# The half-wide pair of a fused attention and double-FFN kernel: operations on two tiles, another product order, one store for two batches

## The chip, the cores and the metric

One core of a Trainium2 chip. The metric is the device time of one execution in microseconds, the median of three runs. The profile is of one further execution of the same program.

## The reference, cut to what matters

All in float32; three stages, the output of each is the input of the next.

```
kv  = einsum('bhsd,bhse->bhde', k, v);  o = einsum('bhsd,bhde->bhse', q, kv)      # batch 8, heads 8, seq 576, dim 64
x   = o / sqrt(mean(o*o, -1) + 1e-6) * g_norm          # as 4608 x 512
x1  = max(x @ w1, x @ w2, x @ w3) @ w_out              # 768 hidden columns
out = (s * relu(x1 @ w_in)**2 + b) @ moe2_w_out        # 2048 hidden columns, 512 out
```

The change lies in the last product, with the `w_out` of the third stage.

## The kernel before, in words

Numbers are kept as pairs of a high and a low part (`hi_part`, a ScalarE copy that rounds, L290; `lo_part`, a VectorE subtraction of that copy from the number, L293), and a product is three matmuls: high by high, high by low, low by high. The two products of the third stage are done with Strassen's method in Winograd's form, with seven products i = 0 to 6 for eight.

The tokens are columns. They are worked on in five pairs of token blocks q; the first four pairs hold two batches' first 512 rows each, in blocks of N = 512 columns. The remaining 64 rows of each of the eight batches (REM = 64) are gathered in a ninth block of 512 columns, and the fifth pair (q = 4) is this block, cut into two halves of 256 columns. `width(q)` says which. This is the half-wide pair. For the last product the work on a pair goes through two halves of the contraction, H = 2q and 2q + 1; so H = 8 and 9 belong to the half-wide pair.

For each H and each of its products i, four steps k of the contraction: `z_load` brings the hidden tiles back from DRAM (`gd`) through SP's queue; `z_sum` makes the sums that products 2 and 3 need, in place, in the tiles of i = 1; `z_hi` and `z_lo` make the high and low part in a slot `zx`, one of six (the tags HS); `z_product` runs 2 x 3 matmuls a step, two output halves m by three part products, into PSUM banks a, b or c (products 0, 2, 4, 6 accumulate in a, 1 and 3 in b, 5 in c). In the half-wide pair a slot holds two steps side by side, 256 columns each, and each m has a bank of its own of which it uses half. `z_comb` takes the banks out: for i < 3 a ScalarE copy, and, where H is odd, VectorE adds what the even H left; for i = 3, 4, 5 VectorE adds bank and copy; for i = 6 it adds to what stands there; at an odd H ScalarE then applies `s` and the bias for each m.

At an odd H, `plan_put` brings the result out. For the first four pairs VectorE transposes a tile in 32 x 32 blocks (`put`, L1255) into one of the four tiles of the rings `t` and `st`, and `put_store` writes it with four DMAs of 64 KB (L1267), each to a destination seen as `a r f` with a = 4 outermost. For the half-wide pair TensorE turns the tile by a product with a unit matrix (`turn_mm`, L1272, for c = 0, 1 and u = 0, 1: tiles named xho and xlo), ScalarE copies it out (`turn_out`, L1277), and `turn_store` (L1282) writes each of the tile's two batches with a DMA of 64 rows by 2 KB, so eight in all; the second of a tile of c = 1 is issued from ScalarE, all others from SP.

The order of the work on every engine is fixed when the program is built. Each piece of work is entered with `job(pos, engine, cost, ...)`: a place in the list, a cost in microseconds, the names that it reads and writes, and the ring slots that it takes. `arrange` plays the list through: an engine takes, of the jobs that are ready when it is free, the one with the lowest place; a job is ready when those that it depends on have ended by the given costs and a lag (2.0 for SP, 0.1 for others, 3.0 for loads). The order so found is what each engine's queue gets; on the chip each engine then runs its queue in that order and waits where it must. `SIZE` gives the slots of a ring. So a cost that is off moves no work on the chip by itself, but changes which work stands before which.

Of the kernel before, what the change touches and what calls it, by code (L numbers as in the profile page):

```python
# [30 lines left out]
def attention_max_ffn_relu2_ffn(ctx: ExitStack, tc, q, k, v, g_norm, w1, w2, w3, wo, wi, w2o, s, b, out):  # L31
# [257 lines left out]
    def hi_part(out, src):  # L289
        act(out=out, in_=src, func=AF.Copy)  # L290
# [566 lines left out]
    def width(q):  # L857
        return N if q < NQ - 1 else N // 2
# [218 lines left out]
    def z_load(H, i, u):  # L1077


        q, n = H // 2, width(H // 2)  # L1080
        parts = (0, 1) if n < N else (H % 2,)
        t = ring("c", f"z_{H}_{u}") if i == 1 else slot(GS[i][u], f"z_{H}_{i}_{u}", F32)
        for e in parts:
            c = slice(e * n, (e + 1) * n) if n < N else slice(0, N)
            k0 = 4 * e
            h = 2 * q + e
            if i == 1:
                p2["z", h, 1, u] = t[:, c]
                nc.sync.dma_start(out=t[:, c], in_=gd[q][:, 3, k0 + u, :n])
                continue  # L1090
            nc.sync.dma_start(out=t[:, :, c], in_=gd[q][:, KEPT[i], k0 + 2 * u:k0 + 2 * u + 2, :n])
            for m in range(2):
                p2["z", h, i, 2 * u + m] = t[:, m, c]

    def z_tile(H, i, k_):
        H0 = H if width(H // 2) == N else H // 2 * 2
        return f"Z{H0}.{i}.{k_ if i == 1 else k_ // 2}"

    def z_key(H, i, k_):
        return f"{z_tile(H, i, k_)}:{0 if i == 1 else k_ % 2}{H % 2}"  # L1100

    def plan_z_load(pos, H, i, u):
        q = H // 2
        k = [u] if i == 1 else [2 * u, 2 * u + 1]
        parts = (0, 1) if width(q) < N else (H % 2,)
        job(pos, SQ_, 0.85 * len(k), z_load, H, i, u, r=[f"gd{q}:{3 if i == 1 else KEPT[i]}.{4 * e + k_}" for e in parts for k_ in k],
            w=[z_key(2 * q + e, i, k_) for e in parts for k_ in k], a=[("c" if i == 1 else GS[i][u], z_tile(H, i, k[0]))], lag=3.0)

    def z_x(H, i, k_):
        return f"ZX{28 * H + 4 * i + (k_ if width(H // 2) == N else k_ // 2 * 2)}:{k_ % 2}"  # L1110

    def z_sum(H, i, k_):
        z = lambda i_: p2["z", H, i_, k_]
        if i == 2:
            tt(nc.vector, z(1), z(1), add, z(0))
        else:
            tt(nc.vector, z(1), z(5), sub, z(1))

    def z_hi(H, i, k_):
        n, o = width(H // 2), 28 * H + 4 * i + k_  # L1120
        if n == N or k_ % 2 == 0:
            st["zx", H, i, k_ // 2] = slot(HS[(o if n == N else o // 2) % M1], f"zx_{o}")
        c = slice(0, N) if n == N else slice(k_ % 2 * n, (k_ % 2 + 1) * n)
        x = hs["z", H, i, k_] = st["zx", H, i, k_ // 2][:, :, c]
        hi_part(x[:, 0], p2["z", H, 1 if 0 < i < 4 else i, k_])

    def z_lo(H, i, k_, eng):
        x = hs["z", H, i, k_]
        lo_part(x[:, 1], p2["z", H, 1 if 0 < i < 4 else i, k_], x[:, 0], nc.gpsimd if eng == G_ else nc.vector)

    def plan_z_right(pos, H, i, k_):
        n, o = width(H // 2), 28 * H + 4 * i + k_
        z = lambda i_: z_key(H, i_, k_)
        if i in (2, 3):
            job(pos, V, cost(V, n), z_sum, H, i, k_, r=[z(0 if i == 2 else 5)], w=[z(1)])
        f, x = z(1 if 0 < i < 4 else i), z_x(H, i, k_)
        new = n == N or k_ % 2 == 0
        job(pos, A, cost(A, n), z_hi, H, i, k_, r=[f], w=[x + "h"],
            a=[(HS[(o if n == N else o // 2) % M1], x.split(":")[0])] if new else [])
        eng = V  # L1140
        job(pos, eng, cost(eng, n), z_lo, H, i, k_, eng, r=[f, x + "h"], w=[x + "l"])

    def z_product(H, i, k_):
        n, new = width(H // 2), i in (0, 1, 5)
        kk = 4 * (H % 2) + k_
        w, x = wt["q", 4 + kk // 2, i], hs["z", H, i, k_]
        for m in range(2):
            if new and k_ == 0:
                st["ps", "z", H, BANK[i], m] = bank(parity(H + (i == 5)), f"zs_{BANK[i]}_{H}_{m}")
            ps = st["ps", "z", H, BANK[i], m][:, :n]  # L1150
            c = slice((2 * (kk % 2) + m) * P, (2 * (kk % 2) + m + 1) * P)
            for e, (a, b_) in enumerate(((0, 0), (0, 1), (1, 0))):
                nc.tensor.matmul(ps, lhsT=w[:, a, c], rhs=x[:, b_], start=new and k_ == 0 and e == 0,  # L1153
                                 stop=k_ == 3 and e == 2, skip_group_check=True)

    def plan_z_product(pos, H, i, k_):
        names = [f"Y{BANK[i]}{H}.{m}" for m in range(2)]
        g = 4 + (4 * (H % 2) + k_) // 2
        job(pos, "PE", 1.365 if width(H // 2) == N else 0.72, z_product, H, i, k_,
            r=[f"WQ{g}.{i}:0", f"WQ{g}.{i}:1", z_x(H, i, k_) + "h", z_x(H, i, k_) + "l"], w=names,  # L1160
            a=[(parity(H + (i == 5)), nm) for nm in names] if i in (0, 1, 5) and k_ == 0 else [])

    def acc(H, i_, m):
        c = int(i_ in (4, 6))
        if ("o", H // 2, c) not in p2:
            tg = ("xh", "xl")[c]
            p2["o", H // 2, c] = base.tile([P, KD, N], F32, tag=tg, name=f"{tg}o_{H}")
        return p2["o", H // 2, c][:, 2 * (i_ in (3, 4)) + m, :width(H // 2)]

    def z_comb(H, i, m, e):  # L1170
        n = width(H // 2)
        ps = st["ps", "z", H, BANK[i], m][:, :n]
        if e == 0:
            st["zc", H, i, m] = ring("s", f"zc_{H}_{i}_{m}")[:, :n]
            act(out=st["zc", H, i, m], in_=ps, func=AF.Copy)
        elif e == 1:
            s_ = st["zc", H, i, m]
            tt(nc.vector, s_, s_, add, acc(H, 5 - i, m))
        elif e == 2:
            tt(nc.vector, acc(H, i, m), ps, add, st["zc", H, 5 - i, m])  # L1180
        elif e == 3:
            tt(nc.vector, acc(H, i, m), ps, add, acc(H, i, m))
        elif e == 4:
            act(out=acc(H, i, m), in_=ps, func=AF.Copy)
        else:
            b_ = 2 * (i in (3, 4)) + m
            act(out=acc(H, i, m), in_=acc(H, i, m), func=AF.Identity, scale=sb_s, bias=p2["bias"][:, b_:b_ + 1])

    def plan_z_combine(pos, H, i):
        n, more = width(H // 2), H % 2  # L1190
        o = lambda i_, m: f"O{H // 2}.{int(i_ in (4, 6))}:{2 * (i_ in (3, 4)) + m}"
        for m in range(2):
            ps = f"Y{BANK[i]}{H}.{m}"
            if i < 3:
                c = f"ZC{H}.{i}.{m}"
                job(pos, A, cost(A, n), z_comb, H, i, m, 0, r=[ps], w=[c], a=[("s", c)])
                if more:
                    job(pos, V, cost(V, n), z_comb, H, i, m, 1, r=[o(5 - i, m)], w=[c])
                continue
            c = int(i in (4, 6))  # L1200
            new = [(("xh", "xl")[c], f"O{H // 2}.{c}")] if not more and m == 0 and i in (3, 4) else []
            e = 2 if i < 6 else 3 if more else 4
            eng = A if e == 4 else V
            job(pos, eng, cost(eng, n), z_comb, H, i, m, e, r=[ps] + ([f"ZC{H}.{5 - i}.{m}"] if e == 2 else []), w=[o(i, m)], a=new)
            if more:
                job(pos, A, cost(A, n), z_comb, H, i, m, 5, r=["bias"], w=[o(i, m)])

# [67 lines left out]
        act(out=o.rearrange("p (a m r) -> p m a r", a=4, m=4), in_=st["turn", c, u].rearrange("p (m a r) -> p m a r", a=4, m=4),  # L1277
            func=AF.Copy)

    def turn_store(c, u, e, eng):  # L1280
        r0 = (4 * c + 2 * u + e) * S_ + N
        (nc.scalar if eng == A else nc.sync).dma_start(out=out[r0:r0 + REM], in_=st["put", c, u][e * REM:(e + 1) * REM])  # L1282

    def plan_put(pos, H, c, u):
        q = H // 2
        tag = either()
        o = [f"O{q}.{c}:{i}" for i in range(4)]
        nm = f"R{H}.{c}.{u}"
        if q < NQ - 1:
            job(pos, V, 0.78, put, H, c, u, tag, r=o, w=[nm], a=[(tag, nm)])  # L1290
            job(pos + 0.05, SQ_, 1.4, put_store, H, c, u, r=[nm])
            return
        job(pos, "PE", 1.0, turn_mm, c, u, r=[*o, "unit"], w=["T" + nm], a=[(parity(u), "T" + nm)])
        job(pos + 0.01, A, 0.65, turn_out, c, u, tag, r=["T" + nm], w=[nm], a=[(tag, nm)])
        for e in range(2):
            eng = A if c and e else SQ_
            job(pos + 0.02, eng, 0.6, turn_store, c, u, e, eng, r=[nm])

# [239 lines left out]
    job(T4 + 28 * (NQ - 1) + 1, G_, 1.0, unit, w=["unit"], a=[("c", "unit")])  # L1540
    for H in range(2 * NQ):
        t = T4 + 14 * H
        order = (0, 5, 1, 2, 3, 4, 6) if H == 2 * NQ - 1 else range(7)
        for n, i in enumerate(order):
            for kk in range(4):
                plan_z_right(t + 2 * n + 0.5 * kk - 3, H, i, kk)
# [37 lines left out]
```

## Time and profile before

| | |
|---|---|
| time, median of 3 runs | 1358.96 us (1358.86 to 1359.13) |
| profiled execution | 1358.27 us |
| its span, first to last instruction | 1356.5 us |
| TensorE (PE) busy | 1336.8 us, 99% of the span |
| VectorE (DVE) busy | 982.4 us, 72% |
| ScalarE (ACT) busy | 788.0 us, 58% |
| mean granted TensorE clock | 0.999 |
| moved by DMA | 251.81 MB, mean 186 GB/s |

The span is the profiled execution from its first to its last instruction; 1.8 us of the execution lie outside of it. Busy shares are means over stages that have different limits; the windows and timelines below cut them into stages.

### The profile page before, as it was taken

The numbers are of one execution on the slowest core, as the hardware profiler recorded it, in microseconds if no ns is written. First come the engines' busy times: TensorE is split into PE (matmuls) and PEld (weight loads), VectorE is DVE, ScalarE is ACT, GpSimd is POOL, SyncE is SP. The second block draws the span as 40 slices with busy tenths as digits, with TensorE's granted clock in tenths as the row PEclk, the third lists the DMA queues.
The fourth block names the chain that finished last, engine by engine and source line by source line (L and its number), as shares of the span: only waits on it lengthen the run. The fifth ranks groups of instructions, "written<-read, shape, count | busy, mean of one in ns | idle before, by whom it ended". The sixth has DMA issues, their size and how long they took to land.

```text
span 1356.5 us, 19727 instructions
## 1 busy us (share of the span) xinstructions
PE 1336.8 (99%) x6948; PEld 1102.0 (81%) x6948; DVE 982.4 (72%) x1671; ACT 788.0 (58%) x1399; POOL 68.1 (5%) x58
## 2 busy tenths in 40 slices
PE   7999999999999999999999999999999999999998
PEld 4777777778888888878888889888888888888888
DVE  4994666767658885477647768658888888888875
ACT  6873555556435453165546567567775656566565
POOL 0001212123110000000000000000000000000000
PEclk9999999999999999999999999999999999999999
DMA  9988988753527638575535645436584464554531
GB/s 267 298 181 210 221 215 224 209 157 95 152 87 249 240 117 267 205 244 184 177 149 196 238 174 169 172 139 223 194 307 151 142 211 142 178 164 138 182 113 48
DMA packets 241010, 251.81 MB, mean 186 GB/s; under 512 B 119184, under 2 KB 177552, under 8 KB 238736
## 3 DMA queue, kind: packets, MB, share of 16 engines
q1 hardware_dynamic: 240752, 250.31, 59.9%
q8 instruction: 54, 0.88, 0.3%
q14 instruction: 44, 0.36, 0.1%
q10 hardware_dynamic: 160, 0.26, 0.1%
HBM read 149.85 MB, written 100.66 MB: 185 GB/s over the span
## 4 chain that ended last, share of the span: by engine, by line
PE 95%; DVE 2%; DMA 1%; SPq 1%; ACT 1%; issue 0%; ACTq 0%; DVEq 0%
PE ps_a L999 15%; PE zs_a L1153 14%; PE g L161 10%; PE g L163 9%; PE g L162 9%; PE ps_b L999 7%; PE fp_a L1392 7%; PE zs_b L1153 7%; PE zs_c L1153 4%; PE ps_c L999 4%; PE fp_b L1392 4%; PE fp_c L1392 2%; PE kvor L348 1%; PE ops L417 1%; PE ms L456 1%; DMA vrem<-in_v_dram 1%
## 5 line engine op out<-in xcount | busy, mean ns | idle before, releaser
L290 ACT ACTIVATE zx<-z 128x512 fp32r<-128x512 f32 (+1 forms) x280 | 158.4, 586 | 122.6 <-PE zs_a L1153 37.8
L1153 PE MATMUL zs_a<-zx,w_q 128*128 128x512 f32 (+1 forms) x960 | 210.9, 368 | 1.0 <-DVE zx L293 1.0
L293 DVE TENSOR_TENSOR zx<-z,zx 128x512 fp32r<-128x512 f32 (+1 forms) x280 | 171.3, 634 | 53.6 <-ACT zx L290 50.2
L999 PE MATMUL ps_a<-x_q,w_q 128*128 128x512 f32 (+1 forms) x960 | 206.0, 368 | 0.0
L1153 PEld LDWEIGHTS zs_a<-zx,w_q 128*128 128x128 f32 x960 | 168.2, 189 | 31.2 <-DVE zx L293 1.2
L999 PEld LDWEIGHTS ps_a<-x_q,w_q 128*128 128x128 f32 x960 | 167.8, 189 | 29.9
L161 PE MATMUL g<-xh,w_w 128*128 128x512 f32 x360 | 142.6, 396 | 0.0
L163 PE MATMUL g<-xh,w_w 128*128 128x512 f32 x360 | 140.4, 390 | 0.7 <-DVE w_w L293 0.7
L162 PE MATMUL g<-xl,w_w 128*128 128x512 f32 x360 | 140.3, 390 | 0.0
L1153 PE MATMUL zs_b<-zx,w_q 128*128 128x512 f32 (+1 forms) x480 | 108.5, 368 | 1.9 <-DVE zx L293 1.9
L999 PE MATMUL ps_b<-x_q,w_q 128*128 128x512 f32 (+1 forms) x480 | 105.1, 368 | 0.0
L1153 PEld LDWEIGHTS zs_b<-zx,w_q 128*128 128x128 f32 x480 | 84.5, 188 | 17.3 <-DVE zx L293 2.3
L999 PEld LDWEIGHTS ps_b<-x_q,w_q 128*128 128x128 f32 x480 | 84.2, 189 | 15.0
L161 PEld LDWEIGHTS g<-xh,w_w 128*128 128x128 f32 x360 | 67.5, 188 | 15.6 <-issue 0.8
L163 PEld LDWEIGHTS g<-xh,w_w 128*128 128x128 f32 x360 | 67.6, 188 | 15.5 <-DVE w_w L293 1.1
L162 PEld LDWEIGHTS g<-xl,w_w 128*128 128x128 f32 x360 | 67.6, 188 | 13.7 <-DVE xl L293 0.3
L576 DVE TENSOR_TENSOR h<-g,h 128x512 f32<-128x512 f32 x60 | 41.5, 691 | 38.5 <-PE g L163 37.3
L1028 ACT ACTIVATE cs<-cs 128x512 f32<-128x512 f32 (+1 forms) x60 | 35.1, 586 | 53.5 <-DVE cs L855 52.8
L1400 ACT ACTIVATE fc<-fp_a 128x512 f32<-128x512 f32 x36 | 21.4, 597 | 68.4 <-PE fp_a L1392 66.0
L1015 ACT ACTIVATE cs<-ps_a 128x512 f32<-128x512 f32 (+1 forms) x80 | 43.4, 555 | 24.9 <-PE ps_a L999 21.0
L1153 PE MATMUL zs_c<-zx,w_q 128*128 128x512 f32 (+1 forms) x240 | 54.1, 368 | 0.0
L855 DVE TENSOR_TENSOR cs<-ps_b,cs 128x512 f32<-128x512 f32 (+1 forms) x40 | 24.9, 637 | 39.5 <-issue 32.5
(325 smaller groups left out, 2498.9 us busy)
## 6 DMA issues: line engine op xcount, KB each, us to landing
z<-gd SPq DMA_DIRECT2D x64, 512.0 KB
gd<-cs SPq DMA_DIRECT2D x96, 256.0 KB
z<-gd SPq DMA_DIRECT2D x48, 256.0 KB
x1d<-x SPq DMA_DIRECT2D x36, 256.0 KB
sd<-fs SPq DMA_DIRECT2D x18, 512.0 KB
raw_w<-in_moe_w_dram SPq DMA_DIRECT2D x18, 511.0 KB
k<-in_k_dram SPq DMA_DIRECT2D x32, 256.0 KB
v<-in_v_dram SPq DMA_DIRECT2D x32, 256.0 KB
```

The source lines that it names most:

```text
L161: nc.tensor.matmul(ps, lhsT=w[:, 0, sl], rhs=xh, start=first, stop=False)
L162: nc.tensor.matmul(ps, lhsT=w[:, 0, sl], rhs=xl, start=False, stop=False)
L163: nc.tensor.matmul(ps, lhsT=w[:, 1, sl], rhs=xh, start=False, stop=last)
L290: act(out=out, in_=src, func=AF.Copy)
L293: eng.tensor_tensor(out=out, in0=src, in1=hi.bitcast(F32), op=ALU.subtract)
L576: nc.vector.tensor_tensor(out=st["h", m], in0=ps, in1=st["h", m], op=ALU.max)
L855: eng.tensor_tensor(out=out, in0=in0, in1=in1, op=op)
L999: nc.tensor.matmul(ps, lhsT=w[:, a, c], rhs=x[:, b_], start=new and k == 0 and e == 0, stop=k == HK - 1 and e == 2, skip_group_check=True)
L1015: act(out=st["cs", G, i, m], in_=st["ps", G, BANK[i], m][:, :n], func=AF.Copy)
L1028: act(out=h, in_=st["ps", G, BANK[i], m][:, :width(q)] if i == 6 else h, func=AF.Relu)
L1153: nc.tensor.matmul(ps, lhsT=w[:, a, c], rhs=x[:, b_], start=new and k_ == 0 and e == 0, stop=k_ == 3 and e == 2, skip_group_check=True)
L1392: nc.tensor.matmul(ps, lhsT=w[:, u, c], rhs=x[:, v_], start=new and k == 0 and e == 0, stop=k == HK - 1 and e == 2, skip_group_check=True)
```

## The change

The half-wide pair only, but for one number.

- `z_load`: for i = 1, a tile holds two steps of one H instead of one step of both, and comes with one DMA in place of two.
- `z_sum`, `z_hi`, `z_lo`: one operation on the two steps k of a slot (128 x 512 elements) in place of two on 128 x 256.
- `z_product`, `z_comb`: both m share one PSUM bank, 256 columns each, and one operation takes both out. The scaling with the bias stays one for each m.
- The product order of H = 8 is 0, 1, 5, 2, 4, 3, 6; it was 0 to 6. That of H = 9 is as before.
- `turn_store`: one DMA a tile for its two batches, four in all; that of c = 1, u = 1 is issued from ScalarE.
- The list's cost of `put_store` is 2.6 for 1.4, that of `turn_store` 0.7 for 0.6. The first holds for all pairs.

```diff
@@ z_load
+            if i == 1 and n < N:
+                if u // 2 == e:
+                    t2 = p2["zp", h, 1, u % 2] = t.rearrange("p (m n) -> p m n", m=2)
+                    nc.sync.dma_start(out=t2, in_=gd[q][:, 3, k0 + u % 2 * 2:k0 + u % 2 * 2 + 2, :n])
+                continue
@@ z_hi
+        if n < N:
+            x2 = st["zx", H, i, k_ // 2]
+            for m in range(2):
+                hs["z", H, i, k_ + m] = x2[:, :, m * n:(m + 1) * n]
+            hi_part(x2[:, 0].rearrange("p (m n) -> p m n", m=2), p2["zp", H, 1 if 0 < i < 4 else i, k_ // 2])
+            return
@@ z_product
-            if new and k_ == 0:
+            if new and k_ == 0 and (n == N or m == 0):
                 st["ps", "z", H, BANK[i], m] = bank(parity(H + (i == 5)), f"zs_{BANK[i]}_{H}_{m}")
-            ps = st["ps", "z", H, BANK[i], m][:, :n]
+            ps = st["ps", "z", H, BANK[i], m] if n == N else st["ps", "z", H, BANK[i], 0][:, m * n:(m + 1) * n]
@@ z_comb
-        ps = st["ps", "z", H, BANK[i], m][:, :n]
+        ps = st["ps", "z", H, BANK[i], m if n == N else 0]
+        if n < N:
+            ps = ps.rearrange("p (m n) -> p m n", m=2)
@@ plan_z_combine
-        for m in range(2):
+        for m in (0, 1) if full else (None,):
@@ turn_store
-    def turn_store(c, u, e, eng):
-        r0 = (4 * c + 2 * u + e) * S_ + N
-        (nc.scalar if eng == A else nc.sync).dma_start(out=out[r0:r0 + REM], in_=st["put", c, u][e * REM:(e + 1) * REM])
+    def turn_store(c, u, eng):
+        to = out.rearrange("(b s) d -> b s d", s=S_)[4 * c + 2 * u:4 * c + 2 * u + 2, N:]
+        (nc.scalar if eng == A else nc.sync).dma_start(out=to, in_=st["put", c, u])
@@ plan_put
-            job(pos + 0.05, SQ_, 1.4, put_store, H, c, u, r=[nm])
+            job(pos + 0.05, SQ_, 2.6, put_store, H, c, u, r=[nm])
...
-        for e in range(2):
-            eng = A if c and e else SQ_
-            job(pos + 0.02, eng, 0.6, turn_store, c, u, e, eng, r=[nm])
+        job(pos + 0.02, A if c and u else SQ_, 0.7, turn_store, c, u, A if c and u else SQ_, r=[nm])
@@ the list
-        order = (0, 5, 1, 2, 3, 4, 6) if H == 2 * NQ - 1 else range(7)
+        order = (0, 5, 1, 2, 3, 4, 6) if H == 2 * NQ - 1 else (0, 1, 5, 2, 4, 3, 6) if H == 2 * NQ - 2 else range(7)
```

## Rows read from the trace of the kernel before

**Rows 1.** Windows: busy us of PE, PEld, DVE, ACT, POOL; clock; DMA share; GB/s.
```profile
34.00:995.00 961.00, 958.78 (x4958) 786.29 (x4958) 672.60 (x1126) 546.01 (x963) 65.86 (x48) 1.00 0.63 194
...
1299.50:1325.00 25.50, 22.56 (x167) 21.16 (x167) 21.70 (x55) 15.73 (x43) 0.00 (x0) 1.00 0.28 83
...
1345.60:1356.50 10.90, 6.23 (x51) 5.76 (x49) 0.79 (x2) 3.90 (x8) 0.00 (x0) 0.91 0.38 96
```

**Rows 2.** Timeline of PE, 1309 to 1319: start, length, work, idle before and its releaser.
```profile
1309.41 2.44 PE L1153 MATMUL zs_a<-zx,w_q 128*128 128x256 f32 x19
1312.86 0.86 PE L1153 MATMUL zs_a<-zx,w_q 128*128 128x256 f32 x5 [1.01 <-DVE zx L293]
1313.56 1.00 PE L1153 MATMUL zs_b<-zx,w_q 128*128 128x256 f32 x7
1315.96 1.57 PE L1153 MATMUL zs_b<-zx,w_q 128*128 128x256 f32 x11 [1.41 <-DVE zx L293]
...
1318.09 0.28 PE L1153 MATMUL zs_b<-zx,w_q 128*128 128x256 f32 x1
1318.90 0.86 PE L1153 MATMUL zs_b<-zx,w_q 128*128 128x256 f32 x5 [0.53 <-DVE zx L293]
```

**Rows 3.** Timeline of DVE: the first and the last of three waiting transposes.
```profile
1311.79 0.71 DVE L1255 STREAM_TRANSPOSE o<-xlo 128x512 f32<-128x512 f32 x1 [0.71 <-DMA out_dram<-o]
...
1317.82 0.71 DVE L1255 STREAM_TRANSPOSE o<-xlo 128x512 f32<-128x512 f32 x1 [0.91 <-DMA out_dram<-o]
```

**Rows 4.** Groups by line and form, 1220 to 1357: count, busy us, mean ns, idle before.
```profile
L293 DVE TENSOR_TENSOR zx<-z,zx 128x512 fp32r<-128x512 f32 x57 | 38.4, 688 | 12.3 <-ACT zx L290 11.4
L290 ACT ACTIVATE zx<-z 128x512 fp32r<-128x512 f32 x57 | 35.2, 630 | 28.0 <-PE zs_a L1153 9.0 <-DVE zx L293 5.8 <-PE zs_b L1153 5.0
...
L293 DVE TENSOR_TENSOR zx<-z,zx 128x256 fp32r<-128x256 f32 x56 | 20.5, 415 | 5.3 <-ACT zx L290 5.0
L290 ACT ACTIVATE zx<-z 128x256 fp32r<-128x256 f32 x56 | 20.1, 411 | 15.7 <-PE zs_a L1153 4.8 <-PE zs_b L1153 4.3 <-issue 2.8
```

**Rows 5.** Timeline of SP's queue: the stores of H = 7.
```profile
1303.04 23.03 SPq L1267 DMA_DIRECT2D out_dram<-o  x32
```

**Rows 6.** DMA view, 1306 to 1324: GB/s in 40 slices; queue's packets, MB, share.
```profile
GB/s 77 69 68 101 72 68 85 83 86 82 84 92 82 86 86 85 86 86 86 86 86 86 86 86 86 86 86 86 86 86 86 86 86 122 88 85 86 86 85 88
...
q1 hardware_dynamic: 3032, 1.51, 28.4%
```

**Rows 7.** DMA view, 1345.6 to 1356.5, slices of 0.27 us: busy tenths, GB/s.
```profile
DMA  0000000039799100000000897979993797900000
GB/s 0 0 0 0 0 0 0 0 90 233 165 233 203 38 0 0 0 0 0 0 0 8 210 225 188 218 188 210 188 346 143 188 180 218 368 8 0 0 0 0
```

**Rows 8.** DMA view, 1266 to 1272: two large loads of `z`.
```profile
DMA  2100000000000000000276569999999620000000
GB/s 82 55 27 0 0 0 0 0 0 0 0 0 0 0 0 0 0 0 0 68 123 109 130 232 335 362 362 341 382 369 382 212 89 0 0 0 0 0 0 0
```

**Rows 9.** Timeline of all engines, 1344 to 1357.
```profile
1344.80 1.05 PE L1272 MATMUL turn<-unit,xho 128*128 128x128 f32 x8
...
1345.61 3.12 PE L1153 MATMUL zs_a<-zx,w_q 128*128 128x256 f32 x24
...
1346.76 6.70 SPq L1282 DMA_DIRECT2D out_dram<-ot  x6
1348.40 0.79 DVE L855 TENSOR_TENSOR xlo<-zs_a,xlo 128x256 f32<-128x256 f32 x2 [2.97 <-PE zs_a L1153]
...
1348.56 1.06 PE L1272 MATMUL turn<-unit,xho 128*128 128x128 f32 x8
1348.86 1.09 ACT L1187 ACTIVATE xlo<-xlo,lim,sb_s 128x256 f32<-128x256 f32 x2 [2.13 <-DVE xlo L855]
...
1351.61 0.58 ACTq L1282 DMA_DIRECT2D out_dram<-ot  x1
1352.36 0.60 ACT L1277 ACTIVATE ot<-turn 128x512 f32<-128x512 f32 x1 [0.79 <-PE turn L1272]
```

More of the change, by code (lines that the diff above doesn't have):

```diff
@@ L1091, in z_load @@
             nc.sync.dma_start(out=t[:, :, c], in_=gd[q][:, KEPT[i], k0 + 2 * u:k0 + 2 * u + 2, :n])
+            if n < N:
+                p2["zp", h, i, u] = t[:, :, c]
             for m in range(2):
@@ L1096, in z_tile @@
         H0 = H if width(H // 2) == N else H // 2 * 2
-        return f"Z{H0}.{i}.{k_ if i == 1 else k_ // 2}"
+        return f"Z{H0}.{i}.{k_ // 2 if i != 1 else k_ if width(H // 2) == N else 2 * (H % 2) + k_ // 2}"
     def z_key(H, i, k_):
@@ L1103, in plan_z_load @@
         q = H // 2
-        k = [u] if i == 1 else [2 * u, 2 * u + 1]
-        parts = (0, 1) if width(q) < N else (H % 2,)
+        half = width(q) < N
+        k = [u] if i == 1 and not half else [2 * (u % 2), 2 * (u % 2) + 1]
+        parts = ((u // 2,) if i == 1 else (0, 1)) if half else (H % 2,)
         job(pos, SQ_, 0.85 * len(k), z_load, H, i, u, r=[f"gd{q}:{3 if i == 1 else KEPT[i]}.{4 * e + k_}" for e in parts for k_ in k],
-            w=[z_key(2 * q + e, i, k_) for e in parts for k_ in k], a=[("c" if i == 1 else GS[i][u], z_tile(H, i, k[0]))], lag=3.0)
+            w=[z_key(2 * q + e, i, k_) for e in parts for k_ in k], a=[("c" if i == 1 else GS[i][u], z_tile(2 * q + parts[0], i, k[0]))], lag=3.0)
     def z_x(H, i, k_):
@@ L1112, in z_sum @@
     def z_sum(H, i, k_):
-        z = lambda i_: p2["z", H, i_, k_]
+        z = lambda i_: p2["z", H, i_, k_] if width(H // 2) == N else p2["zp", H, i_, k_ // 2]
         if i == 2:
@@ L1122, in z_hi @@
             st["zx", H, i, k_ // 2] = slot(HS[(o if n == N else o // 2) % M1], f"zx_{o}")
-        c = slice(0, N) if n == N else slice(k_ % 2 * n, (k_ % 2 + 1) * n)
-        x = hs["z", H, i, k_] = st["zx", H, i, k_ // 2][:, :, c]
+        if n < N:
[4 more added lines that the diff above has]
+            return
+        x = hs["z", H, i, k_] = st["zx", H, i, k_ // 2]
         hi_part(x[:, 0], p2["z", H, 1 if 0 < i < 4 else i, k_])
     def z_lo(H, i, k_, eng):
+        if width(H // 2) < N:
+            hi, lo = (st["zx", H, i, k_ // 2][:, e].rearrange("p (m n) -> p m n", m=2) for e in range(2))
+            lo_part(lo, p2["zp", H, 1 if 0 < i < 4 else i, k_ // 2], hi, nc.vector)
+            return
         x = hs["z", H, i, k_]
@@ L1132, in plan_z_right @@
         n, o = width(H // 2), 28 * H + 4 * i + k_
-        z = lambda i_: z_key(H, i_, k_)
+        if n < N and k_ % 2:
+            return
+        ks = (k_,) if n == N else (k_, k_ + 1)
+        z = lambda i_: [z_key(H, i_, k) for k in ks]
         if i in (2, 3):
[L1135 to L1141, printed above, removed]
+            job(pos, V, 0.69, z_sum, H, i, k_, r=z(0 if i == 2 else 5), w=z(1))
+        f, x = z(1 if 0 < i < 4 else i), [z_x(H, i, k) for k in ks]
+        job(pos, A, 0.62, z_hi, H, i, k_, r=f, w=[x_ + "h" for x_ in x], a=[(HS[(o if n == N else o // 2) % M1], x[0].split(":")[0])])
+        job(pos, V, 0.69, z_lo, H, i, k_, V, r=f + [x_ + "h" for x_ in x], w=[x_ + "l" for x_ in x])
     def z_product(H, i, k_):
@@ L1147, in z_product @@
         for m in range(2):
-            if new and k_ == 0:
+            if new and k_ == 0 and (n == N or m == 0):
                 st["ps", "z", H, BANK[i], m] = bank(parity(H + (i == 5)), f"zs_{BANK[i]}_{H}_{m}")
-            ps = st["ps", "z", H, BANK[i], m][:, :n]
+            ps = st["ps", "z", H, BANK[i], m] if n == N else st["ps", "z", H, BANK[i], 0][:, m * n:(m + 1) * n]
             c = slice((2 * (kk % 2) + m) * P, (2 * (kk % 2) + m + 1) * P)
             for e, (a, b_) in enumerate(((0, 0), (0, 1), (1, 0))):
-                nc.tensor.matmul(ps, lhsT=w[:, a, c], rhs=x[:, b_], start=new and k_ == 0 and e == 0,
+                nc.tensor.matmul(ps, lhsT=w[:, a, c], rhs=x[:, b_], start=new and k_ == 0 and e == 0 and (n == N or m == 0),
                                  stop=k_ == 3 and e == 2, skip_group_check=True)
     def plan_z_product(pos, H, i, k_):
-        names = [f"Y{BANK[i]}{H}.{m}" for m in range(2)]
+        names = [f"Y{BANK[i]}{H}.{m}" for m in range(2 if width(H // 2) == N else 1)]
         g = 4 + (4 * (H % 2) + k_) // 2
@@ L1167, in acc @@
             p2["o", H // 2, c] = base.tile([P, KD, N], F32, tag=tg, name=f"{tg}o_{H}")
+        if m is None:
+            return p2["o", H // 2, c][:, 2 * (i_ in (3, 4)):2 * (i_ in (3, 4)) + 2, :width(H // 2)]
         return p2["o", H // 2, c][:, 2 * (i_ in (3, 4)) + m, :width(H // 2)]
@@ L1171, in z_comb @@
         n = width(H // 2)
-        ps = st["ps", "z", H, BANK[i], m][:, :n]
+        ps = st["ps", "z", H, BANK[i], m if n == N else 0]
+        if n < N:
+            ps = ps.rearrange("p (m n) -> p m n", m=2)
         if e == 0:
-            st["zc", H, i, m] = ring("s", f"zc_{H}_{i}_{m}")[:, :n]
+            st["zc", H, i, m] = ring("s", f"zc_{H}_{i}_{m}")
+            if n < N:
+                st["zc", H, i, m] = st["zc", H, i, m].rearrange("p (m n) -> p m n", m=2)
             act(out=st["zc", H, i, m], in_=ps, func=AF.Copy)
@@ L1189, in plan_z_combine @@
     def plan_z_combine(pos, H, i):
-        n, more = width(H // 2), H % 2
-        o = lambda i_, m: f"O{H // 2}.{int(i_ in (4, 6))}:{2 * (i_ in (3, 4)) + m}"
-        for m in range(2):
-            ps = f"Y{BANK[i]}{H}.{m}"
+        more, full = H % 2, width(H // 2) == N
+        for m in (0, 1) if full else (None,):
+            o = lambda i_: [f"O{H // 2}.{int(i_ in (4, 6))}:{2 * (i_ in (3, 4)) + m_}" for m_ in ((m,) if full else (0, 1))]
+            ps = f"Y{BANK[i]}{H}.{m or 0}"
             if i < 3:
                 c = f"ZC{H}.{i}.{m}"
-                job(pos, A, cost(A, n), z_comb, H, i, m, 0, r=[ps], w=[c], a=[("s", c)])
+                job(pos, A, 0.62, z_comb, H, i, m, 0, r=[ps], w=[c], a=[("s", c)])
                 if more:
-                    job(pos, V, cost(V, n), z_comb, H, i, m, 1, r=[o(5 - i, m)], w=[c])
+                    job(pos, V, 0.69, z_comb, H, i, m, 1, r=o(5 - i), w=[c])
                 continue
             c = int(i in (4, 6))
-            new = [(("xh", "xl")[c], f"O{H // 2}.{c}")] if not more and m == 0 and i in (3, 4) else []
+            new = [(("xh", "xl")[c], f"O{H // 2}.{c}")] if not more and not m and i in (3, 4) else []
             e = 2 if i < 6 else 3 if more else 4
             eng = A if e == 4 else V
-            job(pos, eng, cost(eng, n), z_comb, H, i, m, e, r=[ps] + ([f"ZC{H}.{5 - i}.{m}"] if e == 2 else []), w=[o(i, m)], a=new)
+            job(pos, eng, 0.62 if e == 4 else 0.69, z_comb, H, i, m, e, r=[ps] + ([f"ZC{H}.{5 - i}.{m}"] if e == 2 else []), w=o(i), a=new)
             if more:
-                job(pos, A, cost(A, n), z_comb, H, i, m, 5, r=["bias"], w=[o(i, m)])
+                for m_ in (m,) if full else (0, 1):
+                    job(pos, A, cost(A, width(H // 2)), z_comb, H, i, m_, 5, r=["bias"], w=[f"O{H // 2}.{c}:{2 * (i in (3, 4)) + m_}"])
     def bias_load(g):
```

## The prediction

> **What bounds the kernel now.** I read the windows first. From 34 to 995 us TensorE is busy 958.78 of 961.00 us, and the stages after it up to 1299.5 have no gap at all, so nothing there can be won from another engine. Two places are left: in 1299.5 to 1325 TensorE is busy 22.56 of 25.50 us, and after 1345.6 it is busy only 6.23 of 10.90 us [rows 1]. The clock is not the matter: it is granted in full until the last window.
>
> Then the timeline of TensorE for the first place. It stops three times, each time for VectorE's low part of a `zx` tile [rows 2]. A half-wide matmul starts every 0.12 us (24 of them fill 1345.61 to 1348.56, [rows 9]). So 19 of them from 1309.41 last until 1311.69 and the next starts at 1312.86: 1.17 us lost; in the same way 1.56 us before 1315.96 and 0.69 us before 1318.90, together 3.4 us.
>
> VectorE's timeline tells why: three of its transposes (first and last shown) wait 0.71, 1.08 and 0.91 us for a store of `out` to land, and the `zx` operations queue behind them [rows 3]. The list gave such a store 1.4 us; SP's queue spends 23.03 us on eight of them, 2.9 us each [rows 5], and the ring holds four tiles. While they run, the DMA view is flat at 86 GB/s with 28.4% of the 16 engines in use, although SP issues the next one as fast as it can [rows 6].
>
> **The change part by part.**
>
> Operations on two tiles. In the pair H=8, 9 there are 56 high and 56 low parts of 128x256; 28 and 28 of 128x512 take their place. VectorE: 56 x 0.415 = 23.2 us becomes 28 x 0.688 = 19.3; ScalarE: 56 x 0.411 = 23.0 becomes 28 x 0.630 = 17.6 [rows 4]. The 16 sums and 20 combinations on VectorE halve likewise; at the same durations 36 x 0.415 = 14.9 becomes 18 x 0.688 = 12.4. That is 6.4 us of VectorE, which is not on the path except in the stretch of the three stops, and it pays with latency: high and then low part of the first tile take 1.3 us where 0.83 did.
>
> The product order. For H=8 it becomes 0, 1, 5, 2, 4, 3, 6. Product 5 needs no sum, so it gives VectorE a product's time (24 x 0.12 = 2.9 us) in which to do the late transposes. Its price: a slot of `zx` is (28H+4i+k)//2 mod 6, so products 5 and 2 of H=8 both get slots 2 and 3. Product 2's first tiles can be made only when 5's first two k are done, 0.63 + 0.69 us plus hand-overs, about 1.4 us, beside the 1.44 us that 5's other two k take. That fits with nothing to spare; a transpose that waits for its store there goes straight to TensorE.
>
> The store's time in the list: 2.6 us for 1.4. No instruction comes or goes; the last four transposes move back by 1.2 us a store, near to where their tiles come free. The list still lands each store too early: it gives 2.6 us where 2.9 were seen, and its landing is assumed. So some waiting stays. Of the 3.4 us I take 2.0 as won (bounds: all 3.4, or none).
>
> The loads. For i=1 eight loads of 128 KB become four of 256 KB. SP's last `z` load is out well before 1303.04 [rows 5] and the three stops name no load, so this is worth nothing; were it uncovered, it could only save issues.
>
> PSUM. Both halves of a product share one bank, so one operation reads both and must wait for the second. At the end this costs: now VectorE starts on the first half at 1348.40 while TensorE finishes the second [rows 9]. Then it starts 0.37 us later and takes 0.69 for 0.42: ScalarE's two scalings come 0.6 us later. The fewer banks also free one early for the second turn of `xho`, which now runs at 1348.56 beside the last combination; by its place in the list it goes ahead of product 6 and adds its 0.9 us to TensorE. The first turn and its ScalarE copy are late by some 0.3 us, as product 3's combination takes both halves at once.
>
> The turned stores. This decides. Eight stores of 128 KB become four of 256 KB, one a tile. It saves issues: ScalarE no longer issues a store at 1351.61 between its two last copies, 0.5 us of the 0.79 us idle before 1352.36 [rows 9]. But the destination is now `out` as (batch, row, column) with 2 batches outermost; before it was 64 rows. The rows show two stores that differ in this: the one at L1267, whose destination has 4 outermost, moves 86 GB/s with 28.4% of the engines in use [rows 6], no more than four and a half engines, however many are queued; the present turned stores, with 64 outermost, move 180 to 230 GB/s with nearly all engines busy [rows 7]. I read this as: a store is dealt out over as many engines as its outermost size lets it, and consecutive stores use the same ones. With 2 outermost each engine gets 128 KiB of a store.
>
> The Trainium skill, page "DMA: Bandwidth & Descriptors", section "Why a DMA increments its semaphore by 16 and not by 1", says it outright: a transfer runs on the largest number of engines, at most 16, that divides the slowest dimension above 1 of both sides, and on SP's and ScalarE's queues on the lowest-numbered ones. By it a store of 2 outermost runs on two engines, and ScalarE's store lands on the same two as SP's; no row here shows a store of 2 outermost, nor ScalarE's queue beside SP's on few engines. Without that rule the reading from rows 6 and 7 gives the same two engines.
>
> The price: an engine moves 21.5 GB/s in rows 6 (86 over 4) and 21.3 to 23.9 in the full slices of a large load (341 to 382 over 16, [rows 8]). I take 23.2. Four stores are 4 x 131,072 bytes an engine, 22.6 us (bounds 21.9 to 24.6). They start with the first: its issue at 1346.76 moves by -2.0 + 0.3 to 1345.1, the first bytes come 1.0 us later (1346.76 to the ninth slice of rows 7, 1347.8), so the data ends at 1346.1 + 22.6 = 1368.7. The later stores are issued some 1 and 5 us after the first, always while the two engines are still busy, so what happens to TensorE behind the first store costs and gains nothing any more. From the last bytes to the end of the span it is 1.1 us (1355.4 to 1356.5): 1369.8, which is 13.3 us more than 1356.5. The profiled execution took 1358.27, 0.7 under the median shown; its sum gives 1371.6, and on the median of 1358.96 it is **1372**.
>
> **The rivals.**
>
> All engines (not slower): the lowering deals the store out by the 128 partitions of the source, or by rows. Against it: the store of L1267 has 128 partitions as its source too, and stays at 86 GB/s. Then the path is TensorE's: -2.0 (stops) + 0.9 (second turn) + 0.6 (last combination) - 0.5 (ScalarE's issue) = -1.0, **1358**. It would be below 1356.2 only with all the stops gone and the second turn still behind product 6. It decides at eight engines or more: then a store takes 1.4 us and is under the present tail.
>
> Each store on a pair of its own: two engines a store, but different ones. Against it: the flat 86 GB/s of successive stores. Then only the last store counts: its issue at 1352.99 - 2.0 + 0.9 + 0.6 - 0.5 = 1352.0, bytes from 1353.0, 5.65 us, 1.1 us: 1359.8, 3.3 us more, **1362**.
>
> The stops grow (the change does not do what it says), with all engines: products 5 and 2 share slots, and one transpose that waits between them, 1.1 us as in rows 3, and a `zx` behind it, bring as much as they save, so the 3.4 us stay and the tail's +1.0 comes on top with the slot chain's 1 us: **1361**. For it: the list still sets a landing too early. Under the forecast it only moves the first store, by 2 us, to 1374.
>
> **How the numbers follow.** Forecast 0.82, all engines 0.11 (0.08 within 0.2%, 0.03 faster), own pairs 0.05, stops grow 0.02 (2.0 us, within 0.2%). 0.2% is 2.7 us, about what a measurement of this kernel can tell from no change. Slower: 0.82 + 0.05 = 0.87; same 0.08 + 0.02 = 0.10; faster 0.03. Of the forecast alone the low end is all stops gone and the fastest rate, 1343.4 + 1.0 + 21.9 + 1.1 = 1367.4, 1370 as a time; the high end no gain, the second turn and the slowest rate, 1347.9 + 1.0 + 24.6 + 1.1 = 1374.6, 1377. The engines alone may run faster than in a crowd, so I go down to 1366.
>
> **What would show it.** Right: after about 1350 the DMA view falls to some 45 GB/s at an eighth of the engines, and stays there for over 15 us while all compute engines are done; the last matmul ends near 1350; the chain of waits ends in a DMA of `out<-ot` of more than 10 us. The three stops shrink to some 1.4 us in all. In the timeline the second turn of `xho` stands ahead of the last 24 matmuls. Wrong: 180 GB/s or more at the end and a span under 1360, which means the store is dealt out otherwise than by its outermost size; or a span of 1360 to 1363 with four or more engines busy at once, which means own pairs.

## The result, and the profile after

The changed kernel takes 1373.15 us (median of 4 runs, 1371.11 to 1374.58); before is 1358.91 us in the same comparison. The ratio is 1.0109, 95% interval 1.0096 to 1.0121. The profiled execution took 1371.11 us, the shortest of the four; its span is 1369.3 us.

The windows of the trace after, columns as in [rows 1] (busy us of PE, PEld, DVE, ACT, POOL; clock; DMA share; GB/s), with the stretch from 1351 to 1367.5 beside them:

```profile
1299.50:1325.00 25.50, 23.60 (x179) 22.44 (x178) 21.90 (x36) 13.99 (x23) 0.00 (x0) 1.00 0.27 80
...
1345.60:1369.30 23.70, 4.71 (x37) 4.12 (x35) 0.69 (x1) 2.85 (x6) 0.00 (x0) 0.72 0.12 44
```

```profile
1351.00:1367.50 16.50, 0.73 (x7) 0.54 (x5) 0.00 (x0) 1.07 (x2) 0.00 (x0) 0.65 0.13 51
```

Up to 995 us nothing has changed (from 34 us on TensorE is busy 958.55 of 961.00 us), the stretch of the stops has gained 1.0 us of busy TensorE, and the last stretch is 12.8 us longer. In 16.5 us of it the compute engines have next to nothing left to do (the end of the last turn and its copies: TensorE 0.73 us, ScalarE 1.07 us), while 51 GB/s move at 0.13 of the DMA engines, which is two of sixteen. The DMA view from 1340 on (40 slices of 0.73 us; it answers to [rows 7]), SP's and ScalarE's issues, and what SP waits for at the end of the program:

```profile
DMA  0000000001111111111111111111111111111100
GB/s 0 0 0 0 0 0 0 0 11 28 28 22 45 50 50 50 56 50 50 50 50 50 53 53 50 50 50 50 50 53 53 50 50 50 50 50 53 53 17 0
```

```profile
1345.21 6.80 SPq L1306 DMA_DIRECT2D out_dram<-ot  x3
...
1352.39 1.14 ACTq L1306 DMA_DIRECT2D out_dram<-ot  x1
```

```profile
SPq L1602 <- DMA out_dram<-ot: 16.2, 2, 15.0
```

Before, the same 1.05 MB went at 180 to 230 GB/s [rows 7]. Now the first of the four stores is issued at 1345.21, the rate is 50 GB/s from about 1349 until 1368, and the program's last instructions on SP wait 16.2 us for the stores. The chain of waits does not show this: it ends at ScalarE's copy, and only SP's own waits name the stores.

The stops of TensorE (it answers to [rows 2]) and what stands ahead of the end (to [rows 9]):

```profile
1311.74 3.18 PE L1170 MATMUL zs_a<-zx,w_q 128*128 128x256 f32 x24
1316.73 1.70 PE L1170 MATMUL zs_a<-zx,w_q 128*128 128x256 f32 x12 [1.81 <-ACT zc_None L1198]
...
1343.17 1.95 PE L1296 MATMUL turn<-unit,xho 128*128 128x128 f32 x16
1344.88 3.11 PE L1170 MATMUL zs_a<-zx,w_q 128*128 128x256 f32 x24
```

Three stops have become one. Product 2 ends at 1311.74 + 24 x 0.12 = 1314.62 and product 4, on the same bank, starts at 1316.73: 2.1 us (the row says 1.81, as it counts from the last matmul's end). It waits for ScalarE's copy of the bank. VectorE and then ScalarE around it (it answers to [rows 3]):

```profile
1314.25 0.71 DVE L1279 STREAM_TRANSPOSE o<-xlo 128x512 f32<-128x512 f32 x1 [0.95 <-DMA out_dram<-o]
1314.88 1.25 DVE L855 TENSOR_TENSOR z<-z,z 128x512 f32<-128x512 f32 x2
```

```profile
1315.57 0.63 ACT L290 ACTIVATE zx<-z 128x512 fp32r<-128x512 f32 x1 [1.55 <-DVE z L855]
1316.10 0.58 ACT L1198 ACTIVATE zc_None<-zs_a 128x512 f32<-128x512 f32 x1
```

Read from the bottom up: the copy stands behind a high part, that behind a sum, that behind a transpose that waited for its store to land. It is the wait of before, with another way to TensorE. The second turn of xho stands ahead of the last 24 matmuls, as 16 matmuls in place of 8.

### The profile page after: what moved, and what is told of

It is laid out like the page before. It is cut to its first block, busy times and chain, and to the rows that moved or that the text cites. A ratio compares the mean times of both kernels' runs of the same rounds, so it can differ in the third digit from the quotient of the medians.

```text
span 1369.3 us, 19647 instructions
## 1 busy us (share of the span) xinstructions
PE 1337.8 (98%) x6948; PEld 1103.2 (81%) x6948; DVE 978.8 (71%) x1625; ACT 785.3 (57%) x1364; POOL 68.4 (5%) x58
## 4 chain that ended last, share of the span: by engine, by line
PE 93%; DVE 2%; SPq 2%; DMA 1%; ACT 0%; issue 0%; DVEq 0%
PE ps_a L999 14%; PE zs_a L1170 14%; PE g L161 9%; PE g L162 9%; PE g L163 9%; PE ps_b L999 7%; PE fp_a L1414 7%; PE zs_b L1170 7%; PE ps_c L999 4%; PE fp_b L1414 4%; PE zs_c L1170 3%; PE fp_c L1414 2%; PE kvor L348 1%; PE ops L417 1%; SPq L363 1%; DMA out_dram<-o 1%
## 5 line engine op out<-in xcount | busy, mean ns | idle before, releaser
L290 ACT ACTIVATE zx<-z 128x512 fp32r<-128x512 f32 x252 | 155.6, 630 | 125.0 <-PE zs_a L1170 38.4
L293 DVE TENSOR_TENSOR zx<-z,zx 128x512 fp32r<-128x512 f32 x252 | 169.7, 689 | 53.0 <-ACT zx L290 49.7
```

The source lines that it names most:

```text
L293: eng.tensor_tensor(out=out, in0=src, in1=hi.bitcast(F32), op=ALU.subtract)
```

## The experiments

Each ran beside the kernel before, and ratios are against it. In these profiles the last product starts anywhere from 998.1 to 1001.2 us, so they are compared from the start of its first matmul (998.98 us before, 998.43 after) to the start of its last (A), and from there to the end of the span (B). A and B come from one profile a run. Before, e2, e3 and e10 do the same work in A and read 349.47 to 349.62, and so do after, e1 and e4 with 349.29 to 349.47: a difference of under 0.2 us in A says nothing.

| run | ratio (95% interval) | A, us | B, us |
|---|---|---|---|
| before | 1 | 349.47 | 8.02 |
| after | 1.0109 (1.0096 to 1.0121) | 349.29 | 21.60 |
| e1 eight stores of before | 1.0008 (1.0000 to 1.0017) | 349.43 | 8.88 |
| e2 before, new stores alone | 1.0117 (1.0103 to 1.0131) | 349.53 | 22.64 |
| e3 before, 2 column halves outermost | 1.0131 (1.0117 to 1.0145) | 349.47 | 24.74 |
| e4 changed, rows outermost | 1.0007 (0.9998 to 1.0016) | 349.47 | 8.12 |
| e5 before, transposed tiles' stores by rows | 0.9977 (0.9968 to 0.9986) | 346.71 | 8.02 |
| e6 changed, both kinds by rows | 0.9990 (0.9981 to 0.9999) | 347.91 | 8.12 |
| e7 before, list cost alone | 1.0003 (0.9994 to 1.0012) | 349.62 | 8.01 |
| e8 e1 with the old order | 1.0007 (0.9998 to 1.0016) | 350.33 | 8.89 |
| e9 e6 with the late turn | 0.9984 (0.9975 to 0.9993) | 347.19 | 8.13 |
| e10 before, 4 column quarters outermost | 1.0064 (1.0050 to 1.0078) | 349.62 | 15.47 |
| e11 e5 with one issue off ScalarE | 0.9979 (0.9970 to 0.9987) | 346.71 | 8.20 |
| e12 e9 with the old order | 0.9988 (0.9979 to 0.9997) | 347.61 | 8.14 |

**e1: the changed kernel with the old turned stores.**

```diff
-    def turn_store(c, u, eng):
-        to = out.rearrange("(b s) d -> b s d", s=S_)[4 * c + 2 * u:4 * c + 2 * u + 2, N:]
+    def turn_store(c, u, e, eng):
+        r0 = (4 * c + 2 * u + e) * S_ + N
...
```

> The changed kernel with the eight turned stores of before (64 rows outermost); all else as changed. Theory (the four new stores run on two DMA engines, because 2 is the outermost size of their destination): the tail comes back to before's length. TensorE's stops are then 2.1 us for 3.4, the second turn ahead of product 6 costs 0.9 us, and the last copy waits again for ScalarE's issue: 1358.8 us (1358.2 to 1359.4). Rival (the 14 us come from the shared banks, the order or the wide operations): it stays above 1370 us.

1359.47 us beside 1358.17, ratio 1.0008. B falls from 21.60 to 8.88, 0.86 us above before's: all the rest of the loss was the stores. The rival (shared banks, order, wide operations carry it) falls. The time is a little over what was expected, as a ratio 1.0008 where 0.9999 stood: the rest of the change wins nothing.

**e2: the kernel before with the new stores alone.** The same edit the other way, on the kernel before.

> The kernel before with the four new turned stores alone (two batches outermost, and their list cost). Theory: in the changed kernel the span ended 24.1 us after the first of these stores was issued; here it is issued at 1346.8 us, so the span ends near 1371 us and the time is 1373 us (1371 to 1376), with the DMA view at 50 GB/s for some 20 us. Rival (the compute part carries the loss): 1359 us.

1374.01 us, ratio 1.0117. B is 22.64. The DMA view from 1340 to 1370.7:

```profile
GB/s 0 0 0 0 0 0 0 0 0 11 27 27 27 48 48 51 53 48 53 48 53 51 51 53 48 53 51 51 51 51 53 48 53 51 51 53 48 53 3 0
```

The same flat 50 GB/s. The stores alone make the loss, with nothing else of the change.

**e3: is it the outermost size, or the size and spread of a store?** Eight stores of one batch each, as before, only seen as two column halves. (The source is not cut likewise, so the pieces of these rows come out in other places.)

```diff
-dma_start(out=out[r0:r0 + REM], in_=
+dma_start(out=out[r0:r0 + REM].rearrange("r (a f) -> a r f", a=2), in_=
```

> The kernel before with its eight turned stores of one batch each, but each destination seen as two column halves outermost (1 KB pieces). Theory (the outermost size alone deals the engines out): two engines again, at 22 GB/s each for pieces of 1 KB, 23.5 us of data from the first issue at 1346.8 us: 1374 us (1371 to 1378). Rival (a store is slow because it is 256 KB large or spans two batches that lie far apart): these are small and contiguous in rows, so 1359 us.

1375.83 us, ratio 1.0131. From 1340 to 1373:

```profile
GB/s 0 0 0 0 0 0 0 0 0 15 17 35 38 47 48 48 47 42 35 38 40 42 50 47 50 47 47 50 47 50 47 50 47 48 48 47 50 42 10 0
```

Stores of 128 KB into one run of rows are as slow as those of 256 KB over two batches once 2 stands outermost. The rival falls.

**e4: the same four stores with 64 outermost.** The batches go inside; for that the ninth block's columns are gathered with a pair's batches side by side.

```diff
-        to = out.rearrange("(b s) d -> b s d", s=S_)[4 * c + 2 * u:4 * c + 2 * u + 2, N:]
+        to = out.rearrange("(b s) d -> s b d", s=S_)[N:, 4 * c + 2 * u:4 * c + 2 * u + 2]
-... out=o_rem[:, 2 * u + 1, bb * REM:(bb + 1) * REM] ...
+... out=o_rem[:, 2 * u + 1, bb // 2 * P + bb % 2:(bb // 2 + 1) * P:2] ...
```

> The changed kernel with its four stores of two batches each, but the rows outermost (64) and the batches inside; for that the columns of the ninth block are gathered with the two batches of a pair side by side (strided destination of the small copies early on, same count). Theory (outermost size): all 16 engines, no tail of two engines; the store of ScalarE no longer stands between its last copies, so a little under the kernel with the eight stores: 1358.3 us (1357.3 to 1359.0). Rival (large or far-apart stores are slow): above 1368 us.

1358.72 us, ratio 1.0007. Four stores of 256 KB, and they go at up to 386 GB/s (DMA view, 1342 to 1355.8):

```profile
GB/s 0 0 0 0 0 0 0 0 0 0 0 0 42 368 338 125 380 267 0 0 0 0 0 0 0 0 0 0 0 0 0 350 386 24 386 350 24 0 0 0
```

So one store for two batches is not slow in itself, and the outermost size settles it. ScalarE's last copy, with its issue behind it and not ahead of it:

```profile
1351.78 0.60 ACT L1301 ACTIVATE ot<-turn 128x512 f32<-128x512 f32 x1 [0.29 <-PE turn L1296]
1352.41 0.66 ACTq L1306 DMA_DIRECT2D out_dram<-ot  x1
```

ScalarE is idle for 0.29 us before it where it was 0.79 [rows 9], and B is 0.76 us less than in e1. But the expected gain on before did not come.

**e10: a third size.** As e3, with four quarters (a=4).

> The kernel before with its eight turned stores of one batch each, but each destination seen as four column quarters outermost (512-byte pieces); the output's pieces come out in another place, as the source is not turned with it. Theory (as many engines as the outermost size): four engines, 86 GB/s together; the last five stores are issued within 3 us and hold 0.65 MB, so the end comes some 5 us later: ratio 1.0038 (1.002 to 1.006), between 16 engines (1.0) and two (1.013). Rival (any small outermost size is as slow as two): ratio above 1.008.

1366.35 us, ratio 1.0064, between 16 engines and two; the rival (as slow as two) falls. The number was missed: I had counted the last five stores alone, at the full rate. The view from 1345 to 1364 shows the early ones slow as well, 27 to 61 GB/s for some 3 us, 51 to 85 for the next 4, and only then the 78 to 88 GB/s of four engines:

```profile
GB/s 0 0 0 0 0 0 30 27 40 51 50 61 85 82 75 51 65 77 53 73 83 84 80 78 87 79 86 87 86 86 86 86 88 83 84 68 43 13 0 0
```

**e5: the other store with few engines.** The stores that the stops wait for, with 32 rows outermost in place of 4 column groups; as many, as large.

```diff
-        for j in range(4):
-            r0 = bb * S_ + (u if bb >= ROWS else j) * P
...
-            nc.sync.dma_start(out=to, in_=o[:, j])
+        for a in range(4):
...
+                r0 = bb * S_ + u * P
+                to = out[r0:r0 + P].rearrange("(j r) (a f) -> a r j f", j=4, a=4)[a]
+            nc.sync.dma_start(out=to, in_=o[32 * a:32 * (a + 1)])
```

> The kernel before, but each of the four 64 KB stores of a transposed tile of the full pairs takes one quarter of the partitions with all four row groups (32 rows outermost) instead of all partitions with four column groups outermost. Same count, bytes and 512-byte pieces. Theory (TensorE's three stops come from stores that land late because they run on four engines): the stores land soon after their issue, VectorE's transposes do not wait, the 3.4 us of stops go: 1355.5 us where before is 1358.9 (ratio 0.9975, 0.9968 to 0.9985). Rival (VectorE is simply too busy there): stops stay at 2 us or more, ratio above 0.9988.

1354.94 us beside 1358.13, ratio 0.9977: the lowest of this study, and faster than both kernels. From 1306 to 1324 the DMA view reads mostly 124 to 148 GB/s, where before it is flat at 86 [rows 6]. SP's stores of H = 7 and TensorE's waits from 1295 on:

```profile
1303.59 17.72 SPq L1267 DMA_DIRECT2D out_dram<-o  x32
```

```profile
PE zs_b L1153 <- DVE zx L293: 0.2, 1, 0.2
PE zs_a L1153 <- DVE zx L293: 0.2, 1, 0.2
```

Before, these were 23.03 us [rows 5] and 2.9 us. A is 2.76 us shorter. The rival (VectorE is too busy) falls: its operations are those of before.

**e7: the list's cost alone.**

```diff
-            job(pos + 0.05, SQ_, 1.4, put_store, H, c, u, r=[nm])
+            job(pos + 0.05, SQ_, 2.6, put_store, H, c, u, r=[nm])
```

> The kernel before with the list's cost of a transposed tile's store at 2.6 for 1.4, and nothing else. Theory (stores land some 4 us after their last issue, later than even the new cost says, so transposes still wait, but further back): of the 3.4 us some 1 us is won: ratio 0.9993 (0.998 to 1.0). Rival (a true cost is all that was missing): the stops go, ratio 0.9975.

Ratio 1.0003, A 349.62: nothing won. TensorE's waits for `zx` from 1295 on come to 3.1 us, where they were 2.9. VectorE's transposes:

```profile
DVE o L1255 <- DMA out_dram<-o: 2.9, 3, 1.3
```

Three transposes wait 2.9 us in all, where they waited 2.7. These transposes start 6.1 to 7.1 us after the first of the four issues of the store that they wait for (that of the tile four back); the list allows it 2.6 us and a lag of 2.0. Both expectations were too kind, the rival's more.

**e8: the new order taken back** (range(7) for H = 8, on e1).

> The changed kernel with the eight turned stores of before and with H = 8 in its old order 0 to 6; so the wide operations, the shared bank and the list cost stay. Theory (the new order gives VectorE time for the late transposes): without it the stops are 3 us or more and the time is 1 us above the kernel with the new order (1.0008 of before): ratio 1.0015 (1.0008 to 1.0025). Rival (the order costs, as 2 and 5 share slots and 4 follows 2 on a bank): ratio below 1.0003.

Ratio 1.0007, as e1. The times do not tell the orders apart. The traces do by A, 0.9 us longer with the old order, with four stops (0.3 to 1.0 us idle) where e1 has one (1.9). So for the theory by one trace of each, inconclusive by the time. (e8's profiled run is its slowest, 1362.16 us, mostly because its last product starts 2.8 us later than e1's; A leaves that out.)

**e6: the changed kernel with both kinds of store by rows** (e4 and e5 together).

> The changed kernel with rows outermost in both kinds of store (the four turned stores on 16 engines, as in the run before, and the stores of the transposed tiles as in the run beside this). Theory: the 2.1 us stop before product 4 of H = 8, which goes back to a transpose waiting for its store, goes too: 2.1 us under the kernel that had only the turned stores mended (1.0007 of before), so ratio 0.999 (0.9983 to 0.9997). Rival (the stop is the price of the order, 4 straight after 2 on the same bank): ratio 1.0002 or more.

Ratio 0.9990, as the theory had it. By A it is 1.56 us under e4 and not the whole 2.1, as the stop before product 4 falls to 0.77 us idle and not to nothing:

```profile
1318.04 1.70 PE L1170 MATMUL zs_a<-zx,w_q 128*128 128x256 f32 x12 [0.77 <-ACT zc_None L1198]
```

What is left is the copy itself, between two products on one bank.

**e9: the second turn put back behind product 6** (a later place, and a read of product 6's bank in the list, on e6).

> The changed kernel with rows outermost in both kinds of store, and the second turn of xho put behind product 6 of H = 9 in TensorE's queue, where it stood before the change. Theory (the turn ahead of product 6 adds its 0.9 us to the path): 0.9 us under the run that had both kinds of store mended (0.999 of before): ratio 0.9983 (0.9974 to 0.9991). Rival (the turn only fills the wait for the combination of product 4): ratio 0.999, no change.

Ratio 0.9984, A 0.72 us shorter than in e6, B the same. The turn's place costs 0.7 us; the intervals of e6 and e9 overlap, so it rests on the trace.

**e11: one issue less on ScalarE** (`eng = A if c and u and e else SQ_`, on e5).

> The kernel before with the stores of the transposed tiles with rows outermost, and with only the very last turned store issued from ScalarE (the one that stood between its two last copies goes to SP). Theory: the last copy starts some 0.5 us earlier; ratio 0.9973 (0.9964 to 0.998) where the stores alone gave 0.9977. Rival (SP then has one store more at the end and gives it back): 0.9977 or more.

Ratio 0.9979, which the time can't tell from e5's. ScalarE is idle 0.30 us before its last copy where it was 0.78, so the copy does come earlier; yet B is 8.20 for 8.02. The rival holds: with a seventh store on SP nothing is gained.

**e12: the old order where no store is waited for** (range(7) on e9).

> The run with both stores mended and the late turn, with H = 8 in its old order 0 to 6. Theory (with no store to wait for, the new order only costs: 4 straight after 2 on one bank stops TensorE for 0.9 us): ratio 0.9977 (0.9968 to 0.9984), 0.9 us under the run with the new order. Rival (the new order still serves VectorE, whose sums come early in the old one): ratio 0.9985 or more.

Ratio 0.9988; A is 0.42 us longer than in e9. The theory (then the new order only costs) falls, by A, as the intervals of the two ratios overlap; the new order is worth 0.4 to 0.9 us of TensorE, with 0.8 us of stop of its own included.

One comparison more is in the table. e12 and e5 have the same order, the same place of the second turn and both no store that a transpose waits for; of the change, e12 keeps the wide operations, the joined loads, the shared banks, the list's costs and the four turned stores (rows outermost). Its A is 0.90 us longer and its B 0.12 (the ratios, 0.9988 and 0.9977, overlap). So this part of the change wins nothing even with the wait gone.

## Why the prediction was right, point by point

**The turned stores decide.** Right, with the mechanism: 0.13 of the engines, 50 GB/s, SP's wait for the store. e2 shows it without the rest of the change, e4 and e3 that it is the outermost size, e10 that the loss lies in between with four. The sign of a chain that ends in the store did not come: the chain of waits leaves the stores out, and SP's own waits show them. The Trainium skill, page "DMA: Bandwidth & Descriptors", section "Why a DMA increments its semaphore by 16 and not by 1", gives two engines for 2, and the lowest-numbered ones for SP's and ScalarE's queues. The trace agrees: 0.13 of the engines, and ScalarE's store lay on the same two as SP's, since the rate stays at 50 GB/s when it joins; which two of the sixteen they are it does not show. Both rivals that would have spared the time are refuted.

**The first store's issue.** Forecast 1345.1, seen 1345.21. But that is in part luck: of the 1.55 us that it came earlier than before, 0.55 are the earlier start of the last product in this execution (998.43 for 998.98). The other 1.0 us stands against a forecast of 1.7, as the stops gave back less than 2.0 us.

**The rate.** Forecast 23.2 GB/s an engine; seen 50 to 53 over two, 25 to 26.5, but only after some 2.5 us at 22 to 28 in all. The data took from about 1346.4 to 1368.2, 21.8 us for 22.6: a rate above the one taken and a slow start that I had not foreseen cancel in part. The span came out at 1369.3 for 1369.8. The median, 1373.15, is 1.2 us over the 1372 forecast, within the 3.5 us by which the four runs differ.

**The stops.** The term was mis-sized. I took 2.0 of 3.4 us as won, with 1.4 left; the one stop that is left takes 2.1. A says that TensorE reaches its last matmul 0.2 us earlier (349.29 for 349.47), with the second turn's 0.7 us in it: 0.9 us won. And it was not the list that won it: e7, with the cost alone, waits as long as before, since a store lands later than even the new cost says, and after the change the transposes still wait 2.7 us in all. Step by step, A moves by +0.15 for the list cost (e7, no more than the spread), by +0.7 for the wide operations, shared banks and the turn's place (e8 against e7) and by -0.9 for the order (e1 against e8). The turn's place alone measured 0.72 elsewhere (e6 against e9), so little is left for the wide operations; no run changes them alone. The order won what was won, and the four stops of e8 against the one of e1 fit the reason given.

**The wide operations.** The 6.4 us of VectorE were a wrong reading. I multiplied counts by durations, but operations of one engine overlap: the 56 low parts of 128x256 keep VectorE busy for 20.5 us [rows 4] and not 23.2. From the start of the last product to the end, before and after:

```profile
998.98:1356.50 357.52, 349.91 (x1713) 296.48 (x1711) 288.94 (x496) 217.46 (x396) 0.66 (x2) 1.00 0.48 153
```

```profile
998.43:1369.30 370.87, 349.98 (x1713) 296.54 (x1711) 286.24 (x450) 214.96 (x361) 0.66 (x2) 0.98 0.45 147
```

VectorE is busy 2.7 us less, ScalarE 2.5, and no run shows either on the path.

**The second turn and the last combination.** The turn moved as predicted; 0.9 us was forecast, 0.72 measured, perhaps because it fills a little of the wait between products 4 and 6. The combination over both halves shows in B of e1: 8.88 for 8.02, 0.86 us where 0.6 was forecast. ScalarE's issue: 0.50 of the 0.79 us idle, as forecast (e4), while B fell by 0.76.

**Products 5 and 2 on the same slots.** The chain that I feared fitted: 5 and 2 run without a stop at 1311.74. The stop came one product later, at 4 after 2 on one bank. I had not named that place.

**With all engines** the forecast was 1.0 us under before; e4 is 0.07% above it, interval -0.02 to 0.16. This rival would have been mis-sized by the stops' 1.1 us.

## What to carry to other kernels

Look at the outermost size of both sides of a DMA before joining two into one: here a destination of batch, row, column with 2 batches put a large store on two engines, and the DMA view tells it at once (a flat rate, at 0.13 of the engines for 2 outermost and 0.28 for 4). The same look at the old stores, 4 outermost, gave what the change was after: e5 removes the wait itself, where the changed kernel, with a truer cost in the list, less work on the waiting engine and a better order, has its transposes wait 2.7 us as before. Work that is off the path in the trace (VectorE's 2.7 us) won nothing here, and by A not even when the wait was gone (e12 beside e5).

## What the runs showed that I had not expected

A store on few engines starts slowly: 22 to 28 GB/s for some 2.5 us in the changed kernel and 27 to 28 in e2, and 27 to 61 GB/s for 3 us in e10, before the rates seen later. It looks like the rate of one engine, but two are busy. In the changed kernel (columns as above):

```profile
1346.60:1348.60 2.00, 1.39 (x12) 1.19 (x10) 0.57 (x1) 0.00 (x0) 0.00 (x0) 1.00 0.14 28
```

The share is 0.14, and 0.13 later at 51 GB/s, and the trace has the 2 KB pieces in pairs, side by side, from the first: most take 0.08 us, but about every fourth of an engine 0.27 to 0.42. What holds these up stays open. ScalarE's first issue of a turned store took 1.14 to 1.16 us in the changed kernel, e2, e3 and e10, and 0.56 to 0.66 us in e1 and e4; but its second in e3 took 0.54 us again with data still queued, so the backlog alone does not explain it. The pieces' size counts little beside the number of engines: 25 GB/s an engine at 2 KB (after), 24 at 1 KB (e3), 21.5 at 512 bytes (e10).
